# A decode step on one core: W_Q loaded as two halves from two issuing engines, x behind one of them

## The chip, the cores and the metric

The kernel runs on one core of a Trainium2 chip. The metric is the device time of one execution in microseconds (us); for a version of the kernel it is the median of its runs. A profile is taken of one execution, and its times are counted from the start of the span, which is the time from the first to the last instruction of that execution.

## The reference

A layer norm of x feeds two branches whose outputs are added to x: attention of one new token over a window of cached keys and values, and a gated feed-forward network.

```python
# x (4, 1, 512); k_cache, v_cache (4, 8, 16384, 128); wq (512, 4096); wo (4096, 512)
# w_gate, w_up (512, 1792); w_down (1792, 512); all bfloat16
xn = layernorm(x)
q = (xn @ wq).reshape(4, 1, 32, 128)               # 32 query heads
k, v = the last 4096 positions of the caches       # 8 heads, each used by 4 query heads
p = softmax(q k^T * 128 ** -0.5)
attn = (p v).reshape(4, 1, 4096) @ wo
ffn = (silu(xn @ w_gate) * (xn @ w_up)) @ w_down
out = x + attn + ffn
```

The window of keys and values is 67 MB, W_Q and W_O are 4.2 MB each, and the three matrices of the feed-forward network 1.8 MB each. Everything is read once.

## The kernel before

**Tiling.** The 32 pairs of batch and key head are taken two at a time (two batches, one head), which gives `ND = 16` turns. For one turn K and V are 2 MB each. K has two buffers in `KB`. V has three of the four 2-MB slots of `VQ`; the last two slots of `VQ` hold W_Q (`WQ`) before they hold V.

**A turn.** TensorE transposes the K tiles into PSUM (line 428), ScalarE and VectorE copy them out (lines 325 and 386), TensorE multiplies them by the query (scores, line 415), ScalarE takes the exponential of the turn before (line 329), and TensorE multiplies the probabilities by V. The turns are a loop over registers on each engine, one turn out of step between scores and exponentials.

**The start.** ScalarE loads x as its first instruction (line 310). VectorE waits for it (`d_x`), sums each row (line 341) and counts up `s_xc`. ScalarE and VectorE go on with the layer norm (lines 312 to 345) up to `xn` (line 319); TensorE transposes that in four small steps (line 496), VectorE writes it to SBUF as `XnT` (line 348), and TensorE then waits for W_Q (`d_wq`) and makes the queries in 32 products (lines 502 to 508, carried out in the helper of line 415). VectorE brings the queries into shape (lines 351 and 354), and the first turn begins.

**The order of the loads.** All big loads are issued by SyncE in a fixed order written out by hand in `on_sync`: W_Q (line 287), then a wait for `s_xc`, then K 0, K 1, V 0, W_gate, K 2, V 1, K 3, V 2 and so on, at the end V 15, W_up, W_down and W_O. K load d from 2 on waits until TensorE has transposed all of K load d - 2 (`s_t[1][3]`), V load d from 2 on until VectorE has copied an earlier V (`s_vs[1]`); whatever stands behind such a wait waits too. All but W_Q and x go through the helper `load` (line 190), which reads DRAM in long rows. W_Q is a plain transfer whose view `wq_ap` has 128 rows of 32 KB, one for each partition. SyncE's queue carries W_Q and all later loads; ScalarE's queue carries x at the start and the output at the end.

**The end.** TensorE waits for the pieces of W_O one after another (`out_rows`), then ScalarE and VectorE copy the result out of PSUM (lines 550 and 552), and ScalarE stores it.

Of the kernel before, what the change touches and what calls it, by code (L numbers as in the profile page):

```python
# [12 lines left out]
def bass_parallel_sum__sliding_block_cached__swiglu_ffn__decode_kernel(  # L13
# [13 lines left out]
    _, HKV, Sk, Dh = A_k_cache.shape  # L27
    HQ = A_wq.shape[1] // Dh
# [3 lines left out]
    NC = D // 128  # L32
# [28 lines left out]
    WQ = VQ[:, 2 * KVN:]  # L61
# [65 lines left out]
    def sem(name):  # L127
        return nc.alloc_semaphore(name=name)
    d_x = sem("d_x")
    d_wq = sem("d_wq")  # L130
# [44 lines left out]
    wq_ap = A_wq.rearrange("(p c) n -> p (c n)", c=NC)  # L175
# [10 lines left out]
    def load(eng, to, rows, pieces):  # L186


        with nc.discard():
            by_row = eng.dma_start(to, rows).ins  # L190
        whole = replace(by_row.ins[0], ap=pieces.ap, bass_ap=pieces)
        return eng.add_instruction(replace(by_row, name=nc.get_next_instruction_name(), ins=[whole],
                                           ant_dge_precooked=False))

    def fold_rows(w):
        return w.rearrange("(p c) n -> p (c n)", p=32)

    def load_kv(eng, buf, slot, cache, d):
        return load(eng, buf[:, slot * KVN:(slot + 1) * KVN], kv_ap(cache, d, 1), kv_ap(cache, d, FOLD))

    def both(eng, l, r):
# [2 lines left out]
                              start=False, stop=True, skip_group_check=True)  # L204
        return last

    def heads(c, n):
        return A_wo[c * 128:(c + n) * 128, :]

    def wo_rows(w, n):  # L210
        return w.rearrange("(p c) n -> p (c n)", c=n)
# [64 lines left out]
    def on_sync(eng):  # L276
        def load_k(d):
            if d >= 2:
                eng.wait_ge(s_t[1][NG - 1], d - 1)
            load_kv(eng, KB, d % 2, A_k_cache, d).then_inc(d_k[d % 2], 16)  # L280

        def load_v(d):
            if d >= 2:
                eng.wait_ge(s_vs[1], d - 1)
            load_kv(eng, VQ, d % 3, A_v_cache, d).then_inc(d_v[d % 3], 16)

        eng.dma_start(WQ, wq_ap).then_inc(d_wq, 16)

        eng.wait_ge(s_xc, 1)
        load_k(0)  # L290
        for d in range(1, ND):
            load_k(d)
            load_v(d - 1)
            if d == 1:
                load(eng, WG[:], wg_ap, fold_rows(B_w_gate)).then_inc(d_wg, 16)
        load_v(ND - 1)
        load(eng, WU[:], wu_ap, fold_rows(B_w_up)).then_inc(d_wu, 16)
        load(eng, WD[:], wd_ap, fold_rows(B_w_down)).then_inc(d_wd, 16)
        for j in range(2):
            w = heads(NU + j, 1)  # L300
            load(eng, WO[32 * j:32 * j + 32, NU:NU + NL, :], wo_rows(w, NL),
                 wo_rows(w, 4 * NL)).then_inc(d_wl, 16)
        c = 0
        for q, n in enumerate(WO_RUNS):
            w = heads(c, n)
            load(eng, WO[:, c:c + n, :], wo_rows(w, n), wo_rows(w, n * (2 if n > 8 else 4))).then_inc(d_wo[q], 16)
            c += n

    def before_scalar(eng):
        eng.dma_start(X[:], x_ap).then_inc(d_x, 16)  # L310
        eng.wait_ge(s_xc, 1)
        eng.activation(xc[:], X[:], ACT.Identity, bias=st_neg[:, 0:1], scale=float(D))
        eng.drain()
        eng.activation(xsq[:], xc[:], ACT.Square, accum_out=st_sum[:, 0:1]).then_inc(s_ss, 1)
        eng.wait_ge(s_var, 1)
        eng.activation(st_std[:], st_var[:], ACT.Sqrt).then_inc(s_std, 1)
        eng.wait_ge(s_rs, 1)
        eng.wait_ge(s_const, 1)
        eng.activation(xn[:], xc[:], ACT.Identity, scale=st_rstd[:, 0:1]).then_inc(s_xn, 1)  # L319
# [93 lines left out]
    def on_tensor(eng):  # L413
        def mm(o, l, r, start=False, stop=True):
            return eng.matmul(o, l, r, start=start, stop=stop, skip_group_check=True)  # L415
# [77 lines left out]
        with nc.body("pe_first", valid_engines=PE):  # L493
            eng.wait_ge(s_xn, 1)
            for c in range(NC):
                last = eng.transpose(xT_ps[:, c * B:(c + 1) * B],  # L496
                                     xn[:].rearrange("b (p c) -> b c p", c=NC)[:, c, :], I4[:])
            last.then_inc(s_xT, 1)
            eng.wait_ge(s_xnT, 1)
            eng.wait_ge(d_wq, 16)  # L500

            for n in range(2):
                for c in range(NC):
                    wv = WQ[:, c * HQ * Dh:(c + 1) * HQ * Dh].rearrange("p (n h d) -> p n h d", n=2, d=Dh)
                    for j in range(4):
                        last = mm(ps_q[n][32 * j:32 * j + 32, :].rearrange("p (h d) -> p h d", d=32), XnT[:, c, :],
                                  wv[:, n, :, 32 * j:32 * j + 32], start=(c == 0))
                last.then_inc(s_q, 1)
            eng.wait_ge(s_const, 2)
            eng.br("pe_even")  # L510
# [28 lines left out]
        nc.switch_bb("pe_tail")  # L539

    on_sync(nc.sync)
    before_scalar(nc.scalar)
    before_vector(nc.vector)
    on_gpsimd(nc.gpsimd)
    on_tensor(nc.tensor)
    on_scalar(nc.scalar)
    on_vector(nc.vector)
# [36 lines left out]
```

## Time and profile before

| what | value |
|---|---|
| median of 3 runs | 195.78 us (194.96 to 196.03) |
| the profiled execution, its own time | 195.06 us |
| its span | 193.8 us |
| bytes read | 81.01 MB, 418 GB/s over the span |
| W_Q, issue to landing | 13.9 us |
| K loads, median of 16, issue to landing | 15.1 us |
| V loads, median of 16, issue to landing | 19.4 us |

How to read the profile: PE is TensorE's matmuls, PEld its weight loads, DVE is VectorE, ACT is ScalarE, POOL is GpSimd, SP is SyncE. A name with a q (SPq, ACTq) is the queue of that engine that issues transfers; the time of such a row is that of the issue alone, and the transfer goes on after it. The chain of waits follows the work that ended last back to its start. "Landing" is when the last part of a transfer is in place. In the part on slices, the span is cut into 40 equal pieces of 4.8 us, and a digit is the busy share in tenths; the DMA row is a mean over the core's 16 DMA engines.

### The profile page before, as it was taken

Reading aid. Unit: us, or ns where it says so; the run is one execution under the profiler, and the core shown is the slowest. Engines: PE = TensorE matmul, PEld = TensorE weight load, DVE = VectorE, ACT = ScalarE, POOL = GpSimd, SP = SyncE. Lnnn points to the kernel's source line nnn. Section 1 sums busy time; section 2 is a strip of 40 time slices with the busy share of each in tenths; the row PEclk is TensorE's granted clock in tenths of the full one; section 3 lists DMA queues with packets and bytes.
Section 4 is the critical chain, followed back from the end, with each engine's and each line's share of the span. In section 5 each row is a group of like instructions: output and inputs, shape, how many; then the busy total and the mean of one; then the engine's idle time right before and its main releaser. Section 6 shows DMA issues by size and latency. Waiting matters only on the chain.

```text
span 193.8 us, 7842 instructions
## 1 busy us (share of the span) xinstructions
PE 162.9 (84%) x3529; PEld 142.0 (73%) x3529; DVE 125.8 (65%) x243; ACT 100.5 (52%) x114; POOL 4.3 (2%) x20
## 2 busy tenths in 40 slices
PE   0107999998989898989898989898989898999985
PEld 0102898987878787878787878787878787898752
DVE  1003887777676767676868686868686868689710
ACT  5700476482828282828282828282828282838100
POOL 8000000000000000000000000000000000000000
DMA  6999999999999999999999999999999999998982
GB/s 217 429 429 433 433 514 392 433 433 433 433 433 433 433 433 433 433 433 433 433 433 433 433 433 433 433 433 433 433 433 433 433 433 433 433 490 379 430 361 100
DMA packets 3314, 81.05 MB, mean 418 GB/s; under 512 B 728, under 2 KB 736, under 8 KB 928
## 3 DMA queue, kind: packets, MB, share of 16 engines
q1 hardware_dynamic: 3296, 81.01, 97.4%
q8 instruction: 2, 0.03, 0.1%
q10 hardware_dynamic: 16, 0.01, 0.0%
HBM read 81.01 MB, written 0.00 MB: 418 GB/s over the span
## 4 chain that ended last, share of the span: by engine, by line
DMA 74%; PE 18%; SPq 4%; DVE 1%; issue 1%; DVEq 0%; POOLq 0%
DMA kbuf<-in_A_k_cache_dram 47%; DMA wo_sb<-in_A_wo_dram 16%; PE ps_kt L428 15%; DMA vq<-in_A_v_cache_dram 10%; SPq L190 4%; PE ps_s L415 2%; PE ps_o L415 1%; DMA x_sb<-in_A_x_dram 1%; DVE vq L390 1%; DVE st_neg L341 0%; DVE y_sb L550 0%; PE ps_acc L203 0%; PE ps_mt L415 0%; DVEq L389 0%; DVE vq L389 0%
## 5 line engine op out<-in xcount | busy, mean ns | idle before, releaser
L325 ACT ACTIVATE kT<-ps_kt 128x1024 bf16<-128x1024 bf16 x68 | 66.4, 1034 | 76.5 <-PE ps_kt L428 76.5
L428 PE MATMUL ps_kt<-ident,kbuf 128*128 128x128 bf16 x1088 | 68.1, 222 | 13.5 <-DMA kbuf<-in_A_k_cache_dram 13.5
L428 PEld LDWEIGHTS ps_kt<-ident,kbuf 128*128 128x128 bf16 x1088 | 62.3, 99 | 20.4 <-DMA kbuf<-in_A_k_cache_dram 16.2
L386 DVE COPY kT<-ps_kt 128x1024 bf16<-128x1024 bf16 x68 | 46.6, 691 | 15.4 <-PE ps_kt L428 14.3
L415 PE MATMUL ps_o<-p,vq 128*128 128x64 bf16 x1088 | 35.4, 193 | 0.0
L415 PEld LDWEIGHTS ps_o<-p,vq 128*128 128x128 bf16 x1088 | 34.7, 98 | 0.7
L415 PEld LDWEIGHTS ps_s<-qs,kT 128*128 128x128 bf16 x1088 | 32.4, 98 | 3.9 <-issue 3.9
L415 PE MATMUL ps_s<-qs,kT 128*128 128x64 bf16 (+3 forms) x1088 | 33.9, 191 | 0.0
L389 DVE COPY vq<-vq 128x4096 bf16 x17 | 20.8, 1226 | 8.5 <-POOLq L274 8.5
L325 ACT ACT_TABLE_LOAD x17 | 21.8, 1283 | 0.3
L390 DVE COPY vq<-vq 128x4096 bf16 x17 | 20.8, 1221 | 0.0
L379 DVE TENSOR_REDUCE m<-ps_mt 8x1 f32<-8x128 f32 x17 | 4.7, 279 | 11.9 <-PE ps_mt L415 11.9
L392 DVE TENSOR_REDUCE rm<-ps_s 128x8 bf16<-128x512 f32 x17 | 11.6, 684 | 0.0
L329 ACT ACTIVATE p<-ps_s 128x512 bf16<-128x512 f32 x17 | 10.2, 603 | 0.0
L361 DVE TENSOR_REDUCE den<-ps_o 128x8 f32<-128x256 f32 x18 | 7.3, 406 | 1.1 <-PE ps_o L415 1.1
L415 PE MATMUL ps_s<-vq,xnT 128*32 128x512 bf16 x16 | 1.9, 625 | 6.8 <-DMA vq<-in_A_wq_dram 6.8
L496 PE MATMUL ps_acc<-i,xn 4*128 4x4 f32 x4 | 0.6, 261 | 7.4 <-ACT xn L319 7.4
L415 PE MATMUL ps_s<-mkc,mkr 2*128 2x512 bf16 x17 | 6.5, 385 | 0.0
L415 PE MATMUL ps_s<-dg,ones 8*128 8x512 bf16 x17 | 6.5, 385 | 0.0
L415 PE MATMUL ps_o<-p,ones 128*128 128x256 bf16 x34 | 6.4, 270 | 0.0
L351 DVE STREAM_TRANSPOSE wo_sb<-ps_s 128x512 f32<-128x512 f32 x1 | 0.7, 717 | 8.5 <-PE ps_s L415 8.5
L496 PEld LDWEIGHTS ps_acc<-i,xn 4*128 4x128 f32 x4 | 0.5, 207 | 7.4 <-ACT xn L319 7.4
(74 smaller groups left out, 59.6 us busy)
## 6 DMA issues: line engine op xcount, KB each, us to landing
kbuf<-in_A_k_cache_dram SPq DMA_DIRECT2D x16, 2048.0 KB, 15.1
vq<-in_A_v_cache_dram SPq DMA_DIRECT2D x16, 2048.0 KB, 19.4
vq<-in_A_wq_dram SPq DMA_DIRECT2D x1, 4096.0 KB, 13.9
wo_sb<-in_A_wo_dram SPq DMA_DIRECT2D x1, 2048.0 KB, 31.5
wg_sb<-in_B_w_gate_dram SPq DMA_DIRECT2D x1, 1792.0 KB, 28.2
wu_sb<-in_B_w_up_dram SPq DMA_DIRECT2D x1, 1792.0 KB, 25.3
wd_sb<-in_B_w_down_dram SPq DMA_DIRECT2D x1, 1792.0 KB, 28.8
wo_sb<-in_A_wo_dram SPq DMA_DIRECT2D x8, 128.0 KB, 32.3
```

Of the source, the lines that this page charges most:

```text
L190: by_row = eng.dma_start(to, rows).ins
L325: eng.activation(KT[:, h * HKN + 1024 * g:h * HKN + 1024 * (g + 1)], kt_ps[g].rearrange("p a b -> p (a b)"), ACT.Copy).then_inc(s_e[h][g], 1)
L329: eng.activation(P[:, 0:SN], ps_S[:], ACT.Exp, scale=SCALE).then_inc(s_p, 1)
L361: eng.tensor_reduce(den[:], den_ps.rearrange("p (t c) -> p c t", c=C), AX.X, ALU.add)
L379: eng.tensor_reduce(m8[:], mt_ps, AX.X, ALU.max)
L386: eng.tensor_copy(KT[:, h * HKN + 1024 * g:h * HKN + 1024 * (g + 1)], kt_ps[g].rearrange("p a b -> p (a b)")).then_inc(s_e[h][g], 1)
L389: eng.tensor_copy(VS[:, 0:HKN], VQ[:, ds(at, HKN)]).then_inc(s_vs[0], 1)
L390: eng.tensor_copy(VS[:, HKN:], VQ[:, ds(at + HKN, HKN)]).then_inc(s_vs[1], 1)
L392: eng.tensor_reduce(RM[:], ps_S[:].rearrange("p (t c) -> p c t", c=C), AX.X, ALU.max).then_inc(s_rm, 1)
L415: return eng.matmul(o, l, r, start=start, stop=stop, skip_group_check=True)
L428: last = eng.transpose(kt_ps[g][:, k, :], KB[:, a:a + 128], ident[:])
L496: last = eng.transpose(xT_ps[:, c * B:(c + 1) * B], xn[:].rearrange("b (p c) -> b c p", c=NC)[:, c, :], I4[:])
```

## The change

W_Q is loaded by two transfers in place of one. Each takes half of every partition's 32 KB, so each has 128 rows of 16 KB. The first half is SyncE's first instruction, the second half ScalarE's first instruction; x, until now the first instruction of ScalarE, is issued behind that half on the same queue. Both halves count up `d_wq`, and TensorE waits for 32 in place of 16. SyncE's wait for `s_xc` and all loads behind it are as before.

```diff
+    def load_q(eng, h):
+        n = NC * HQ * Dh // 2
+        eng.dma_start(WQ[:, h * n:(h + 1) * n], wq_ap[:, h * n:(h + 1) * n]).then_inc(d_wq, 16)
+
...
     def on_sync(eng):
...
-        eng.dma_start(WQ, wq_ap).then_inc(d_wq, 16)
+        load_q(eng, 0)
 
         eng.wait_ge(s_xc, 1)
         load_k(0)
...
     def before_scalar(eng):
+        load_q(eng, 1)
         eng.dma_start(X[:], x_ap).then_inc(d_x, 16)
         eng.wait_ge(s_xc, 1)
...
             eng.wait_ge(s_xnT, 1)
-            eng.wait_ge(d_wq, 16)
+            eng.wait_ge(d_wq, 32)
```

## The prediction

> **What bounds the kernel now.** I read the page from the DMA rows, then the chain of waits, then the first 30 us in order of time. The busy rows and slices come first.
>
> ```profile
> span 193.8 us, 7842 instructions
> PE 162.9 (84%) x3529; PEld 142.0 (73%) x3529; DVE 125.8 (65%) x243; ACT 100.5 (52%) x114; POOL 4.3 (2%) x20
> ...
> DMA  6999999999999999999999999999999999998982
> GB/s 217 429 429 433 433 514 392 433 433 433 433 433 433 433 433 433 433 433 433 433 433 433 433 433 433 433 433 433 433 433 433 433 433 433 433 490 379 430 361 100
> ...
> q1 hardware_dynamic: 3296, 81.01, 97.4%
> q8 instruction: 2, 0.03, 0.1%
> q10 hardware_dynamic: 16, 0.01, 0.0%
> ...
> DMA 74%; PE 18%; SPq 4%; DVE 1%; issue 1%; DVEq 0%; POOLq 0%
> ```
>
> TensorE is busy 84% of the time, but the DMA row stands at 9 in every slice but the first and the last few, near 433 GB/s, and 74% of the chain that ended last is DMA. The kernel is one stream of 81 MB on SyncE's queue (q1), with no pause after the first microseconds. Its speed, from the chain in order of time:
>
> ```profile
> 0.80 1.74 DMA x_sb<-in_A_x_dram
> 2.54 0.02 issue
> 2.56 0.69 DVE st_neg L341
> 3.25 0.02 issue
> 3.27 16.28 DMA kbuf<-in_A_k_cache_dram
> 19.55 0.05 issue
> 19.59 3.44 PE ps_kt L428 x32
> ...
> 52.22 15.14 DMA kbuf<-in_A_k_cache_dram
> ...
> 71.61 15.14 DMA kbuf<-in_A_k_cache_dram
> ...
> 191.75 0.30 PE ps_acc L203 x2
> 192.04 0.02 issue
> 192.07 0.41 DVE y_sb L550
> ```
>
> Between the K loads of 52.22 and 71.61 lie 19.39 us and four loads of 2.097 MB: 4.85 us a load, 432.5 GB/s. The stages that matter are two: how early the stream starts and whether it ever runs dry. The same view tells what holds the second instruction of the stream: x is issued at 0.80, lands at 2.54, VectorE sums it (0.69), and only then, at 3.27, may SyncE issue K load 0. Today that wait costs nothing, as W_Q's 4 MB still lie ahead of K 0. The windows show it; columns are the stretch, its length, the busy time of five engines, the clock, the DMA share and GB/s:
>
> ```profile
> 0.00:12.00 12.00, 0.64 (x4) 0.55 (x4) 1.14 (x4) 6.21 (x8) 4.33 (x20) 1.00 0.86 347
> 12.00:14.70 2.70, 0.00 (x0) 0.00 (x0) 0.00 (x0) 0.00 (x0) 0.00 (x0) 1.00 1.05 449
> 14.70:19.60 4.90, 3.61 (x33) 1.25 (x33) 1.75 (x4) 0.00 (x0) 0.00 (x0) 1.00 0.99 428
> 19.60:190.00 170.40, 156.73 (x3469) 139.21 (x3471) 122.48 (x235) 93.87 (x105) 0.00 (x0) 1.00 1.00 431
> ```
>
> In the first 12 us 12 x 347 = 4.16 MB move, so W_Q (4.194 MB) is through, on the mean of the 16 DMA engines, at 12.07. At 432.5 GB/s it needs 9.70 us, so the data began at 2.37, 1.57 us after the issue. Beyond 12 the rate goes on at 449: K 0 follows without a gap. The rows of the two first transfers:
>
> ```profile
> vq<-in_A_wq_dram SPq DMA_DIRECT2D x1, 4096.0 KB, 13.9
> ...
> 0.80 0.39 SPq L287 DMA_DIRECT2D vq<-in_A_wq_dram  x1
> 0.80 0.56 ACTq L310 DMA_DIRECT2D x_sb<-in_A_x_dram  x1
> ```
>
> W_Q is reported landed at 0.80 + 13.9 = 14.7, that is 2.6 us behind the mean: some DMA engine runs late. That late one stays: the stream's mean end is 2.37 + 81.01/0.4325 = 189.7, and TensorE waits for the last piece until 191.75, 2.0 later.
>
> **The change part by part.**
>
> Moved on ScalarE: x goes from first to second place. Its issue costs some 0.4 us more (SyncE's W_Q row, 0.39, for the instruction ahead of it), which is hidden by what follows: behind 2 MB on ScalarE's own queue, x can't land before that half is through. Where both queues are served alike, the half that ScalarE issued ends when SyncE's does, with the whole of W_Q. The earliest landing is then 0.80 + 1.74 (x's own time in the row) + 9.70 = 12.24. The latest is with the last part of W_Q, 14.7. By q10's row, x and the output, two transfers of four rows, have 16 packets, eight each: x lies on a few of the 16 DMA engines, not on all, so it need not meet the late one. I take 12.9, a good quarter of the way.
>
> The Trainium skill ("DMA: Bandwidth & Descriptors", section "Queues, rings and completion order") says that each DMA engine takes the descriptors of one queue in order and changes between queues packet by packet, in turns. By that x is among the last packets of W_Q, which gives the landing I take; the trace of before has no two long queues side by side that could show it.
>
> What the moved x delays: s_xc comes 0.73 after the landing (0.02 + 0.69 + 0.02), at 13.63, and behind that wait on SyncE's queue stand all loads of K, V and the weights. Nothing is left in either queue by then, so the cover that made the wait free is gone. K 0 issued at 13.63 brings data 1.57 later, at 15.20; W_Q was through at 12.07. The stream stands still for 15.20 - 12.07 = 3.13 us. Bounds: 2.47 with x at 12.24, and 4.93 with x at 14.7.
>
> By the same page ("Latency and other measured facts") a transfer issued from SyncE brings its first byte after about 0.6 us; the pause would be some 1.0 shorter and the time near 197.3. The row of W_Q has 1.57, and x took 1.74 to land with only 4 KB, so I stay with the row.
>
> What the pause gives back: DMA engines that run late work on in it, while the others stand, and all of them start K 0 together. At most the 2.0 us by which the last piece trails the mean is won, at least nothing, as the restart may spread them again just as the first start did (2.6 at W_Q). I take 0.75, below the half, because the spread at W_Q appeared within one start.
>
> Added: 128 more rows, half as long. The nearest rows are those of the last weights, 128 KB in 4-KB rows, one after another:
>
> ```profile
> 191.09 0.09 PEld L203 LDWEIGHTS ps_acc<-wo_sb,oS 128*4 128x4 bf16 x2 [0.18 <-DMA wo_sb<-in_A_wo_dram]
> 191.42 0.09 PEld L203 LDWEIGHTS ps_acc<-wo_sb,oS 128*4 128x4 bf16 x2 [0.24 <-DMA wo_sb<-in_A_wo_dram]
> 191.75 0.09 PEld L203 LDWEIGHTS ps_acc<-wo_sb,oS 128*4 128x4 bf16 x2 [0.24 <-DMA wo_sb<-in_A_wo_dram]
> ```
>
> 0.33 each where 432.5 GB/s would give 0.303: 0.027 for two rows on each DMA engine, 0.014 a row. Eight more rows a DMA engine: +0.11; bounds 0 and 0.11.
>
> Two issues side by side: both queues issued at 0.80 before as well, and W_Q's data still came after 1.57. I take no gain; the bound is the half of 1.57 if that time were spent on making one list of rows, -0.8.
>
> TensorE and VectorE behind x. From these rows:
>
> ```profile
> 8.10 0.17 DVE L348 CAST xnT<-ps_acc 128x16 bf16<-128x16 f32 x1 [1.62 <-PE ps_acc L496]
> ...
> 14.84 1.90 PE L415 MATMUL ps_s<-vq,xnT 128*32 128x512 bf16 x16 [6.78 <-DMA vq<-in_A_wq_dram]
> 16.50 1.94 PE L415 MATMUL ps_o<-vq,xnT 128*32 128x512 bf16 x16
> ...
> 25.27 0.53 SPq L190 DMA_DIRECT2D kbuf<-in_A_k_cache_dram  x1
> ```
>
> x to xnT takes 8.27 - 2.54 = 5.73, the query products 18.44 - 14.84 = 3.60. Today xnT is ready 6.6 before W_Q; after the change it ends last: 12.9 + 5.73 = 18.6, products until 22.2 (before 18.44). K 0's mean end is 15.20 + 4.85 = 20.1 and its last part at most 2.6 later, so the first turn hangs on the query, 3.8 later than now at most, and K load 2, which waits for that turn, is issued near 25.27 + 3.8 = 29.1. The queue holds K 0, K 1, V 0 and W_gate until then: 12.32 MB with W_Q, today through at 2.37 + 28.5 = 30.9, then at 34.0. With 1.57 to start, K 2 must be issued before 32.4: 3.3 us to spare. No second pause. If that cover were gone, each microsecond over it would cost one. The wait for 32 in place of 16 on d_wq has no price: W_Q is long there by 18.6. The table load of ScalarE moves behind two issues, and x comes at 12.9, so it is hidden.
>
> **Sum.** 3.13 + 0.11 - 0.75 = 2.5 us longer. The profiled execution took 195.06 (span 193.8 and 1.26 around it): 197.6. It lies 0.7 under the median of 195.78 shown, and the runs to be predicted are medians: 198.3.
>
> **The rivals.**
> 1. Faster. ScalarE's queue is served ahead of SyncE's, and each queue makes its own half of the list of rows. Then x lands at 0.80 + 1.74 + 4.85 = 7.4, K 0 is issued at 8.1 and can follow by 9.7, while W_Q is in work until 11.3 (12.07 less 0.8): no pause, and the stream is 0.8 to 1.6 earlier, 194.2 to 195.0. The point that decides: x in before some 9.0. For it: in the first 12 us 1.0 MB less moves than at the steady rate. Against it: that loss was there though two queues were issued from. The Trainium skill's same page ("Issuing engines are not separate DMA queues") says that a second issuing engine saves only the sequencer's time to issue; that speaks against this rival, and here the saving would be part of SyncE's 0.39.
> 2. No change: x early as there, the start as now. 195.8.
> 3. The pause swallows the lateness wholly: 2.47 - 2.0 to 3.13 - 2.0, so 196.3 to 196.9. For it speaks the 2.0 us tail; against it, that a start spread the DMA engines by 2.6.
> 4. x falls on the late DMA engine, or the restart spreads them anew: pause 4.93, little given back: 199.7 to 200.7.
>
> **How the numbers follow.** My case (rise of 1.0 to 3.8) 0.64; rival 4, 0.15; rival 3, 0.09, half of it under the bound of what can be told; rival 2, 0.06; rival 1, 0.06, a sixth of it too small to tell. About 0.5% (1.0 us) is what the runs can tell from no change. Slower: 0.64 + 0.15 + 0.05 = 0.84; same 0.04 + 0.06 + 0.01 = 0.11; faster 0.05. The range leaves out rivals 1 and 2 and the top of rival 4: 196.4 to 200.4.
>
> **What would show it.** Right: the chain of waits has x landing between 12 and 15, K 0 issued 0.7 behind it, the DMA row dips in the third or fourth slice (9.7 to 19.4), the later slices stand as before, the last weights some 2.5 later. The wait of TensorE ahead of the query products is on xnT, not on W_Q. Wrong: x in before 9, or a full DMA row between 12 and 15, or K 2 issued later than 32 with a second dip behind it. A first W_Q half that is through much before 12 would overturn the even sharing.

## The result and the profile after

The changed kernel takes 198.26 us (median of 4 runs, 198.08 to 198.55) beside 195.37 for the kernel before (median of 4, 194.73 to 196.03). The ratio of the runs is 1.0173 with a 95% interval of 1.0152 to 1.0195: slower by 1.7%, some 3.4 us. The two medians alone are 2.9 us apart, because two of the four runs before took about 196 us; the runs of the kernel before that were taken beside the experiments have medians of 194.8 to 194.9, and from there the rise is 3.4. The forecast said 198.3 us and slower. The profiled execution took 198.55, its span 197.3. Two runs of a later version (x first on ScalarE), over 1.5% slower than its fastest, are left out of its figures.

The page of the changed kernel, in the same order as before:

```profile
span 197.3 us, 7843 instructions
...
DMA  6958999999999999999999999999999999999793
GB/s 216 429 213 319 425 445 458 425 425 425 425 425 438 478 445 438 432 425 425 425 425 425 425 425 425 425 445 478 445 438 425 425 425 425 425 399 558 319 413 120
...
q1 hardware_dynamic: 3296, 78.91, 93.5%
q10 hardware_dynamic: 160, 2.11, 2.6%
...
DMA 63%; PE 25%; SPq 4%; DVE 3%; issue 2%; ACT 1%; DVEq 0%; ACTq 0%; POOLq 0%
```

The third slice (9.9 to 14.8) has fallen from 9 to 5 and from 429 to 213 GB/s, the fourth to 319; from the fifth on the row is as full as before. TensorE's share of the chain is up from 18% to 25%, which is a trap: it looks as if TensorE had become the bound. The chain in order of time tells why it has not:

```profile
1.25 12.09 DMA x_sb<-in_A_x_dram
13.36 0.69 DVE st_neg L346
...
22.35 0.72 DVE wo_sb L356
...
55.09 14.50 DMA kbuf<-in_A_k_cache_dram
...
73.84 15.14 DMA kbuf<-in_A_k_cache_dram
...
195.23 0.30 PE ps_acc L203 x2
```

x lands at 13.36 in place of 2.54. From there the chain goes through the layer norm, the queries and the first turns until 55, because the turns start late and for a while run back to back; meanwhile the DMA row stays full, and from 55 on the chain goes over the K loads again, as in the kernel before. The windows of the changed kernel show the pause itself:

```profile
0.00:12.00 12.00, 0.00 (x0) 0.00 (x0) 0.00 (x0) 1.28 (x1) 4.33 (x20) 1.00 0.87 344
12.00:14.70 2.70, 0.00 (x0) 0.00 (x0) 0.67 (x1) 0.63 (x1) 0.00 (x0) 1.00 0.10 38
14.70:19.60 4.90, 1.25 (x12) 0.85 (x16) 0.47 (x3) 4.30 (x7) 0.00 (x0) 1.00 0.86 321
19.60:192.00 172.40, 157.10 (x3484) 137.94 (x3477) 123.76 (x238) 93.97 (x105) 0.00 (x0) 1.00 1.00 433
```

Until 12 us almost nothing differs (344 against 347 GB/s): two queues brought W_Q no sooner. From 12.0 to 14.7 the rate is 38 against 449 GB/s. How much of the stream that cost, over the first 20 us, first the kernel before, then the changed one:

```profile
0.00:20.00 20.00, 4.65 (x41) 2.20 (x42) 3.19 (x9) 6.21 (x8) 4.33 (x20) 1.00 0.94 389
```
```profile
0.00:20.00 20.00, 1.65 (x16) 1.01 (x20) 1.14 (x4) 6.21 (x8) 4.33 (x20) 1.00 0.78 307
```

20 x (389 - 307) = 1.64 MB less, which is 3.8 us at 432.5 GB/s. The instructions behind it, in order of time:

```profile
14.06 1.26 SPq L190 DMA_DIRECT2D kbuf<-in_A_k_cache_dram  x2
...
18.76 0.17 DVE L353 CAST xnT<-ps_acc 128x16 bf16<-128x16 f32 x1 [1.48 <-PE ps_acc L501]
18.98 0.14 PEld L420 LDWEIGHTS ps_s<-vq,xnT 128*32 128x32 bf16 x8 [0.35 <-DVE xnT L353]
...
29.10 0.54 SPq L190 DMA_DIRECT2D kbuf<-in_A_k_cache_dram  x1
```

K 0 is issued 0.70 after x has landed; the query products now wait for xnT and no more for W_Q; K 2 goes out at 29.10.

### The profile page after: what moved, and what is told of

Read it like the earlier page. It is cut to its first block, busy times and chain, and to the rows that moved or that the text cites. A ratio compares the mean times of both kernels' runs of the same rounds, so it can differ in the third digit from the quotient of the medians.

```text
span 197.3 us, 7843 instructions
## 1 busy us (share of the span) xinstructions
PE 161.2 (82%) x3529; PEld 140.3 (71%) x3529; DVE 125.3 (64%) x243; ACT 100.6 (51%) x114; POOL 4.3 (2%) x20
## 4 chain that ended last, share of the span: by engine, by line
DMA 63%; PE 25%; SPq 4%; DVE 3%; issue 2%; ACT 1%; DVEq 0%; ACTq 0%; POOLq 0%
DMA kbuf<-in_A_k_cache_dram 30%; DMA wo_sb<-in_A_wo_dram 17%; PE ps_kt L433 15%; DMA vq<-in_A_v_cache_dram 10%; DMA x_sb<-in_A_x_dram 6%; PE ps_s L420 5%; SPq L190 4%; PE ps_o L420 4%; DVE vq L395 1%; ACT xn L324 0%; ACT xc L317 0%; ACT xsq L319 0%; DVE wo_sb L356 0%; DVE st_neg L346 0%; PE ps_acc L501 0%
## 5 line engine op out<-in xcount | busy, mean ns | idle before, releaser
L433 PE MATMUL ps_kt<-ident,kbuf 128*128 128x128 bf16 x1088 | 66.6, 219 | 12.0 <-DMA kbuf<-in_A_k_cache_dram 10.8
L433 PEld LDWEIGHTS ps_kt<-ident,kbuf 128*128 128x128 bf16 x1088 | 60.8, 98 | 18.6 <-DMA kbuf<-in_A_k_cache_dram 13.0
L346 DVE TENSOR_REDUCE st_neg<-x_sb 4x1 f32<-4x512 bf16 x1 | 0.7, 674 | 13.4 <-DMA x_sb<-in_A_x_dram 13.4
L317 ACT ACTIVATE xc<-x_sb,st_neg 4x512 f32<-4x512 bf16 x1 | 0.7, 721 | 10.9 <-DVE st_neg L346 10.9
## 6 DMA issues: line engine op xcount, KB each, us to landing
vq<-in_A_wq_dram ACTq DMA_DIRECT2D x1, 2048.0 KB, 12.1
```

The costliest lines, as they stand in the source:

```text
L433: last = eng.transpose(kt_ps[g][:, k, :], KB[:, a:a + 128], ident[:])
```

## The experiments

Times are medians; each ratio is against runs of the kernel before on the same chip (medians there 194.8 to 194.9). Theory A is that of the prediction: SyncE's queue runs dry because K 0 waits for an x that lies behind ScalarE's half.

**x behind W_Q without halves or a second queue.** ScalarE's issue of x removed, and in SyncE's list:

```diff
         eng.dma_start(WQ, wq_ap).then_inc(d_wq, 16)
+        eng.dma_start(X[:], x_ap).then_inc(d_x, 16)
```

> The kernel before with one W_Q transfer of 32-KB rows on SyncE's queue, and x issued by SyncE behind it; no second queue and no halves. Theory A: x lands between 12.3 and 14.7, K 0 is issued 0.7 later, and the time is that of the changed kernel, 198.3 within 0.8. Theory B: with the halves gone the time is that of before, 195.4.

Measured 198.25, ratio 1.0157 (1.0127 to 1.0187), as the changed kernel. Its chain and its windows:

```profile
1.28 11.70 DMA x_sb<-in_A_x_dram
```
```profile
0.00:12.10 12.10, 0.00 (x0) 0.00 (x0) 0.00 (x0) 1.28 (x1) 4.32 (x20) 1.00 0.86 344
12.10:15.80 3.70, 0.00 (x0) 0.00 (x0) 0.82 (x2) 2.00 (x4) 0.00 (x0) 1.00 0.32 90
```

x lands at 12.98 and the same hole follows (90 GB/s between 12.1 and 15.8). One long transfer ahead of x on the same queue does all of the harm; the halves and the second queue aren't needed for it.

**Both halves on SyncE, x alone and first on ScalarE.**

```diff
         load_q(eng, 0)
+        load_q(eng, 1)
...
     def before_scalar(eng):
-        load_q(eng, 1)
```

> Two halves of W_Q with 16-KB rows, both issued by SyncE, x alone and first on ScalarE. Theory A: 195.4, at most 0.2 more for 128 further rows. Theory B with the rows as the cause: 197 to 198.3. Beside the run with x first on ScalarE it gives the worth of the second queue, which I expect to be under 0.5.

Measured 194.77, ratio 0.9996 (0.9974 to 1.0018). The 16-KB rows cost nothing that can be told, so theory B falls as far as it names the rows.

**The order of ScalarE's two issues turned.**

```diff
     def before_scalar(eng):
-        load_q(eng, 1)
         eng.dma_start(X[:], x_ap).then_inc(d_x, 16)
+        load_q(eng, 1)
```

> The halves stay on two queues; only the order of ScalarE's two issues is turned, x first. Theory A (SyncE's queue runs dry, because K 0 waits for x behind ScalarE's half): x lands near 2.5, K 0 is issued near 3.3, no dip beyond 12 us, and the time is that of the kernel before, 195.4 within 0.7. Theory B (two queues or 16-KB rows make the stream slower): the time stays near 198.3.

Measured 196.0 (195.27 to 197.52), ratio 1.0059 (1.0032 to 1.0086). Most of the loss is gone, but not all, and neither theory had said that. The profile (an execution of 195.49) names the rest. Its transfers, then its time order, then its window from 30 to 34, and last the same window of the kernel before:

```profile
vq<-in_A_wq_dram ACTq DMA_DIRECT2D x1, 2048.0 KB, 17.9
```
```profile
19.46 1.90 PE L420 MATMUL ps_s<-vq,xnT 128*32 128x512 bf16 x16 [11.72 <-DMA vq<-in_A_wq_dram]
...
29.43 0.53 SPq L190 DMA_DIRECT2D kbuf<-in_A_k_cache_dram  x1
```
```profile
30.00:34.00 4.00, 4.00 (x128) 3.86 (x125) 2.70 (x5) 1.77 (x2) 0.00 (x0) 1.00 0.81 307
```
```profile
30.00:34.00 4.00, 4.00 (x64) 3.42 (x61) 3.35 (x9) 3.23 (x5) 0.00 (x0) 1.00 0.90 389
```

ScalarE's half lands at about 19.3, although W_Q as one transfer was there at 14.7. With x early, K 0 sits on SyncE's queue right behind SyncE's half and shares the DMA engines with ScalarE's half. The query products start at 19.46 in place of 14.84, K 2 is issued at 29.43 in place of 25.27, and the stream thins there (307 against 389 GB/s). So the second queue has a price of its own: a load that isn't needed yet gets ahead of one that is. Beside the run with both halves on SyncE (194.77) that price is 1.2 us, where under 0.5 had been expected.

**The wait ahead of K 0 taken out of the changed kernel.**

```diff
         load_q(eng, 0)
-        eng.wait_ge(s_xc, 1)
         load_k(0)
```

> The changed kernel without SyncE's wait for s_xc ahead of K 0; x stays behind ScalarE's half. Theory A: x lands at 12.5 to 14 as in the changed kernel, but the stream has no pause, so the time is 195.0 to 196.2 although the queries come as late (products until about 22.3). Theory C (what costs is the late query chain, by which TensorE's first turns end 4 us later): about 198.3, as without this edit.

Measured 197.47, ratio 1.0130 (1.0094 to 1.0165): about three quarters of the loss stays. Both theories were too simple. Chain, time order and windows:

```profile
1.25 14.13 DMA x_sb<-in_A_x_dram
```
```profile
31.43 0.54 SPq L190 DMA_DIRECT2D kbuf<-in_A_k_cache_dram  x1
```
```profile
12.00:16.00 4.00, 0.00 (x0) 0.00 (x0) 0.60 (x1) 0.00 (x0) 0.00 (x0) 1.00 1.03 443
```
```profile
30.00:32.00 2.00, 2.00 (x39) 1.67 (x36) 1.70 (x3) 1.46 (x2) 0.00 (x0) 1.00 0.14 57
```

The first pause is gone (443 GB/s from 12 to 16). But x lands later still, at 15.38, the turns start later, K 2 goes out at 31.43, and the queue, which by the prediction's sum is through at 30.9 when there is no pause, runs dry there: 57 GB/s from 30 to 32. The second pause takes the place of the first. In the changed kernel itself the first pause of 3.8 us pushed that date to about 34.7 and thereby hid the late turns.

**Whose turn: rows or bytes.** ScalarE gets a quarter of every row (8 rows of 8 KB on each DMA engine) in place of a half.

```diff
-        n = NC * HQ * Dh // 2
+        n = NC * HQ * Dh * 3 // 4
+        w = slice(0, n) if h == 0 else slice(n, NC * HQ * Dh)
-        eng.dma_start(WQ[:, h * n:(h + 1) * n], wq_ap[:, h * n:(h + 1) * n]).then_inc(d_wq, 16)
+        eng.dma_start(WQ[:, w], wq_ap[:, w]).then_inc(d_wq, 16)
```

> The changed kernel with W_Q divided by columns: ScalarE has a quarter of every row (8 KB, 8 rows on each DMA engine), SyncE three quarters (24 KB, 8 rows). The same bytes on ScalarE's queue as with 32 whole rows. If the queues take turns row by row, ScalarE's last row is still among the last of W_Q, x lands at 12 to 13.5 and the time is near 198.3. If the queues share by bytes, x lands near 7.5 and the time is 195.4.

Measured 198.27, ratio 1.0150 (1.0104 to 1.0196). x, behind half as many bytes, is as late as ever:

```profile
1.25 12.19 DMA x_sb<-in_A_x_dram
```

So the queues take turns row by row here, whatever the rows hold.

**The same rule turned to use.** SyncE's half goes out in four transfers with 4-KB rows; ScalarE's half and x behind it stay.

```diff
         n = NC * HQ * Dh // 2
-        eng.dma_start(WQ[:, h * n:(h + 1) * n], wq_ap[:, h * n:(h + 1) * n]).then_inc(d_wq, 16)
+        m = n if h else n // 4
+        for o in range(h * n, (h + 1) * n, m):
+            eng.dma_start(WQ[:, o:o + m], wq_ap[:, o:o + m]).then_inc(d_wq, 16)
...
-            eng.wait_ge(d_wq, 32)
+            eng.wait_ge(d_wq, 80)
```

> The changed kernel, but SyncE's half of W_Q goes out as four transfers with rows of 4 KB (32 rows on each DMA engine); ScalarE's half (8 rows of 16 KB) and x behind it are as they were. If the queues take turns row by row, ScalarE's half is through after 8 turns of 20 KB, near 2.4 + 6.1 = 8.5; x lands near 9.5, K 0 is issued near 10.2 and brings data near 12, when W_Q runs out: no pause to speak of, 195.2 within 0.7, with x still behind ScalarE's half. If the queues share by bytes, x lands near 13 and the time is near 198.3.

Measured 196.56 (195.49 to 197.10), ratio 1.0076 (1.0054 to 1.0098). Chain, time order and windows (of an execution of 195.54):

```profile
1.25 8.68 DMA x_sb<-in_A_x_dram
```
```profile
10.65 1.26 SPq L190 DMA_DIRECT2D kbuf<-in_A_k_cache_dram  x2
```
```profile
0.00:12.00 12.00, 0.00 (x0) 0.00 (x0) 0.67 (x1) 2.56 (x4) 4.33 (x20) 1.00 0.85 326
```

x lands at 9.93, close to the 9.5 expected, still behind 2 MB, and about half of the loss is gone (1.8 us are left, against 194.79 for the kernel before): the place of x is confirmed as the main cause by changing nothing but how SyncE's half is cut. The time missed its band by 0.7. The first 12 us run at 326 in place of 347 GB/s, 0.25 MB or 0.6 us, which fits the profiled execution (195.54). The runs themselves fall into two groups, 195.5 to 195.8 and 196.4 to 197.1; what makes the upper one is open.

**W_Q cut by partitions: 96 rows on SyncE, 32 on ScalarE.**

```diff
-        n = NC * HQ * Dh // 2
-        eng.dma_start(WQ[:, h * n:(h + 1) * n], wq_ap[:, h * n:(h + 1) * n]).then_inc(d_wq, 16)
+        w = slice(32, 128) if h == 0 else slice(0, 32)
+        eng.dma_start(WQ[w, :], wq_ap[w, :]).then_inc(d_wq, 16)
```

> The changed kernel with W_Q divided by partitions: ScalarE issues 32 rows of 32 KB, SyncE 96. Each DMA engine has 2 of ScalarE's rows and 6 of SyncE's. If the queues take turns row by row, x comes behind 4 rows of 1.21 us: at 2.4 + 4.9, that is near 7.5; K 0 is issued near 8.3 and follows W_Q without a pause: 195.4 within 0.8. If a queue is emptied by its own share of bytes in step with the other, x lands near 12 to 13 and the time is near 198.3.

Measured 204.23, ratio 1.0455 (1.0408 to 1.0503). The time is neither of the two expected and tells nothing about turns, since the cut itself halves the speed of W_Q: the trace has a record of every row that is moved, and by these a 32-KB row of W_Q, the first on each DMA engine left out, takes 2.0 to 2.5 us, where it mostly takes 1.21 in the kernel before. The control puts two transfers of 96 and 32 rows on SyncE's queue, with x first on ScalarE. Its cut is not at the same place: the first transfer has partitions 0 to 95 and the second 96 to 127, where the run above had 32 to 127 on SyncE and 0 to 31 on ScalarE.

```diff
-        n = NC * HQ * Dh // 2
-        eng.dma_start(WQ[:, h * n:(h + 1) * n], wq_ap[:, h * n:(h + 1) * n]).then_inc(d_wq, 16)
+        w = slice(96, 128) if h else slice(0, 96)
+        eng.dma_start(WQ[w, :], wq_ap[w, :]).then_inc(d_wq, 16)
...
         load_q(eng, 0)
+        load_q(eng, 1)
...
     def before_scalar(eng):
-        load_q(eng, 1)
```

> W_Q cut by partitions (96 and 32 rows of 32 KB) as in the run that took 204.2, but both transfers on SyncE's queue, and x alone and first on ScalarE. If the cut itself makes W_Q slow (217 GB/s in the first 12 us there), W_Q still lands near 19 to 22 and the time is 200 to 202. If two queues at once were the cause, W_Q lands near 14.6 and the time is 195.

Measured 205.20, ratio 1.0502 (1.0454 to 1.0550), above the 200 to 202 expected. The first windows of the two:

```profile
0.00:12.00 12.00, 0.00 (x0) 0.00 (x0) 0.00 (x0) 1.28 (x1) 4.32 (x20) 1.00 0.91 217
```
```profile
0.00:12.00 12.00, 0.64 (x4) 0.55 (x4) 1.14 (x4) 6.21 (x8) 4.33 (x20) 1.00 0.94 215
```

215 to 217 GB/s with one queue as with two, at a DMA share over 0.9: two queues aren't needed for it. What the two runs share is the cut by partitions, and the two halves by columns on SyncE's queue (194.77) show that it isn't the number of transfers. Why the cut costs that much is open.

**Where the given-back time went.** By the chains, the K loads in the middle land 2.23 later than before (55.09 + 14.50 = 69.59 against 52.22 + 15.14 = 67.36; 88.98 against 86.75). The stream as a whole is 3.8 late, so 1.6 was given back, as the late DMA engines worked on in the pause. By the trace a K load lands in 16 parts, one for each DMA engine, and the records of these landings have the parts of K 0 within 0.36 us of one another, before within 2.19. Two engines were late before. As far as the times of the single transfers tell which follows which, they are those that also carried the two 16-KB transfers of the instruction queue (q8) while W_Q was loading, 0.92 and 0.96 us each. The full stream never made up for that: the parts of the last V load still landed 2.13 apart. But the last weights come 195.23 - 191.75 = 3.48 later: most of it is lost again at the end. Theory T: the two small loads of W_O's last rows (8 pieces of 16 KB each) lie on a part of the DMA engines, not on the late ones. Before, the late ones set the end and the small loads are hidden in their lateness; after the pause all are level, and those with the small loads end last (in the same records of the changed kernel, eight of the 16 are 1.2 us behind the other eight after the next load). First the loads were spread over 16 pieces, in both kernels:

```diff
-                 wo_rows(w, 4 * NL)).then_inc(d_wl, 16)
+                 wo_rows(w, 2 * NL)).then_inc(d_wl, 16)
```

> The changed kernel with the two small loads of the last W_O rows read in 16 pieces of 8 KB in place of 8 pieces of 16 KB. In the changed kernel the K and V loads in the middle land 2.2 us later than before, the last piece of W_O 3.5 later. Theory T (after the pause all DMA engines are level, and the two small loads, which lie on a part of them, put that part behind again by about two pieces of 0.61 us): spread over all, the end comes 0.4 to 0.8 earlier, about 197.6. Otherwise: no change, 198.3.

> The same edit on the kernel before, where some DMA engines already run about 2 us late from the start. Theory T: those late ones get up to 0.6 us more to carry, and the end comes 0 to 0.6 later, 195.4 to 196.0. If the edit is a gain by itself, 194.8.

Measured 198.54 (1.0171; 1.0135 to 1.0207) for the changed kernel: no gain, a miss. And 196.67 (1.0082; 1.0057 to 1.0107) for the kernel before, a larger loss than either case had. The direction of the second is that of T, its size is not, and a piece of half the size does not cost half (0.31 to 0.60 us in the records, where the 16-KB pieces took 0.615), so the pair decides little. Then both loads left out, a memset in their place:

> The changed kernel without the two small loads of W_O's last rows (GpSimd fills their place with zeros, so the share of the last two heads in the output is left out). Theory T (in the changed kernel the DMA engines that carry these two loads end last, two pieces of 0.61 us behind the others): the end comes 1.0 to 1.3 earlier, 197.1. Rival (they do not set the end; it is the length of the whole stream): 0.26 MB less at 432.5 GB/s, 0.6 earlier, 197.7.

> The same part left out of the kernel before. Theory T (there the end is set by DMA engines that run late from the start and carry none of these two loads): 0 to 0.5 earlier, 194.5 to 194.9, so that the distance between the two kernels shrinks from 3.4 to about 2.4. Rival: 0.6 earlier as in the other, and the distance stays near 3.4.

Measured 197.43 (1.0126; 1.0101 to 1.0151) and 194.81 (0.9990; 0.9976 to 1.0005). The changed kernel gains 0.8, between T's 1.0 to 1.3 and the rival's 0.6, which alone doesn't decide; the kernel before gains nothing, where the rival wanted 0.6. The distance falls from 3.4 to 2.6, close to the 2.23 of the middle. T is supported, and by these medians it accounts for 0.8 of the 1.25 that the end takes back. The landing records of the profiled executions give it more: in the changed kernel eight parts of the last piece of W_O are in place by 193.92 and the other eight only between 194.86 and 195.19, while before the last part lands at 191.70. From 191.70 to 193.92 are 2.22, the distance of the middle, so in these two executions the eight engines with the small loads account for all that the end takes back.

## Why the prediction was right

The sign, the places and the mechanism of the loss were as forecast; the part that the pause gives back was not. Right, step by step:

- x among the last of W_Q: taken 12.9, measured 13.36, within the bounds of 12.24 and 14.7. The turns between the queues, which the trace of before couldn't show, are shown by the quarter of columns and the short rows. The Trainium skill ("DMA: Bandwidth & Descriptors", "Queues, rings and completion order") has turns packet by packet; in these runs a turn is a whole row, be it of 4, 8, 16 or 24 KB, as x's landings at 13.36, 13.44 and 9.93 tell.
- s_xc 0.73 later and K 0 behind it: 0.70.
- No gain from two issues side by side: 344 against 347 GB/s until 12 us. It speaks against rival 1, as does x's landing at 13.36. The Trainium skill's rule (same page, "Issuing engines are not separate DMA queues") agrees with that row.
- The late queries hidden: products from 18.98 (18.6 said), K 2 at 29.10 (29.1 said), no second pause. That this cover is real and how thin it is, the run without the wait showed: there the queue was through near 30.9 by the prediction's sum, K 2 came at 31.43, and the loss was 2.5 us.
- 128 more rows: 0.11 taken; with both halves on SyncE the interval is -0.26% to +0.18% (-0.5 to +0.35 us), so nothing contradicts it, but it is too small to be told.

Where terms were mis-sized: the pause was put at 3.13 and is 3.8. Of the difference, x's landing has 0.46; the rest is the restart, about 1.9 from the issue of K 0 until the stream is back in place of W_Q's 1.57; the 1.9 is worked back from the 3.8, with W_Q through near 12.15 at 344 GB/s (12.15 + 3.8 - 14.06). The Trainium skill's 0.6 us (same page, "Latency and other measured facts") is for the first byte alone. The records come near it if one counts from the end of the issue: W_Q's first row starts at 1.84, 0.65 after its issue ends at 1.19. The start of the stream takes longer because the first rows are slow: 1.3 to 2.2 us for W_Q and 1.2 to 2.3 for K 0, where later ones take 1.21.

The time given back was put at 0.75: it is 1.6 in the middle and 0.3 at the end. The reason given for 0.75, that a start spreads the DMA engines anew, does not hold. The restart left them within 0.36 us, and the lateness before goes with the two instruction transfers rather than with the start. In the middle of the run the pause swallowed nearly all of the lateness, which was the mechanism of rival 3; what made the end later again, the small loads of W_O, the prediction didn't have at all. That 0.75 lies between 1.6 and 0.3 is luck.

Sum: 3.8 - 0.3 = 3.5 between the profiled executions (198.55 and 195.06), where 2.5 was forecast; it lies within the 1.0 to 3.8 given to the case.

That the time came out at 198.26 for a forecast of 198.3 is so in part because two errors cancel. The sum was set on the median of three runs, 195.78; more runs put the kernel before at 194.8 to 195.4. The base was 0.4 to 0.9 too high and the rise too low by as much. The profiled execution's own 195.06 was the better base.

No version that computes the whole output ran faster than the kernel before; with both halves on SyncE it is the same.

## What to carry to other kernels

In a kernel that, like this one, is one saturated stream of loads, look at what the issuing engine waits for and whether enough bytes are queued ahead of that wait; a 4-KB transfer that releases the stream must not be queued behind megabytes, on whatever queue. A second queue added no speed to the full stream here but changed the order, row for row: it can put a small or urgent transfer last, and it lets loads that aren't needed yet pass one that is. When a pause is taken away, find the date of the next one (here the issue of K 2) before counting the gain.

## What the runs showed of the hardware that was not expected

- W_Q cut by partitions into 96 and 32 rows of 32 KB came at 215 to 217 GB/s over the first 12 us, at partition 32 with two queues and at partition 96 with one, where the transfer over all 128 partitions has 347. The runs don't show why.
- Two long transfers on two queues alternate by rows and not by bytes: with 8-KB rows ahead of x against 24-KB rows on the other queue x landed at 13.44, with 16 against 16 at 13.36, and with 16 against 4 at 9.93.
- DMA engines that fall behind in a full stream stay behind: the parts of K 0 landed within 2.19 us and those of the last V load, 154 us later, within 2.13. A pause of 3.8 us levelled them to 0.36 (1.6 us given back in the middle of the run), and the tail can hang on which of them carry the odd small loads (eight parts 1.2 us behind the other eight).
